# Two transposed tiles of the combine weights, moved from the expert stage to the start of the feed-forward stage

## The chip, the cores and the metric

The kernel runs on one core of a Trainium2 chip. The metric is the time of one execution on the device in microseconds (us), lower is better. Beside the timed runs there is one profiled execution, from which all rows of the trace come. TensorE is PE in the rows (PEld for its weight loads), VectorE is DVE, ScalarE is ACT, GpSimd is POOL, and SP issues the transfers.

## The reference

```python
x = attention(q, k, v)            # 4 batches, 8 heads, 576 tokens, head size 64; banded masks
# x: 2304 tokens x 512
logits = x @ phi                  # 2304 x 32 slots (8 experts, 4 slots each)
d = softmax(logits, axis=0); slot_input = d.T @ x
h = relu(slot_input[e] @ w1[e]);  slot_out[e] = h @ w2[e]       # for each expert e
c = softmax(logits, axis=1)       # the combine weights, 2304 x 32
x = c @ slot_out                  # 2304 x 512
h = x @ w_in                      # 512 -> 2048
r = relu(h);  g = r * r
out = g @ w_out                   # 2048 -> 512
```

## The kernel before

The order of the instructions on every engine is written out by hand, in two strings of tokens: `ATT` for the attention stage and the routing, `SEQ` for the rest. A loop at the end takes `SEQ` token by token and calls the function of each; an engine does its instructions in the order in which they were called. The letters behind a token say which engine does it (`A` ScalarE, `V` VectorE).

**Expert stage.** `y` multiplies a w1 tile (`L736`), `x` a w2 tile (`exp2`, `L859`); each tile is a transfer of 1 MB. `so` copies an expert group's result out of PSUM (`L873`), `sel` transposes it (`L764`) and copies it into `sT` (`L767`), which holds `slot_out` transposed.

**Feed-forward stage.** It never forms `c @ slot_out`. It forms M = `slot_out @ w_in` (32 rows) and then h = c @ M, by chunks of 128 columns of the 2048. So that the product keeps its precision in the fast format, the combine weights and M are held in three row groups, high parts and low parts: `C3` is the transposed combine weights, 96 rows, and M has 96 rows too.

- `cp ca.A cv` makes one of the eight tiles of `C3`, 288 columns each: `cp` three transposes on TensorE into a PSUM tile (`L702`), `ca` the copy into `C3` (`L713`), `cv` the subtraction that leaves the low part in rows 64 to 95 (`L718`, VectorE). The tiles 0 to 3 form `C3a`, the others `C3b`. After each `cp` GpSimd lays out the next tile's input in three copies (`L690`).
- `iM.0` to `iM.4` turn chunk M of w_in from 64 to 32 bits (`L806` or `L808`, `L812` on ScalarE, `L815`, `L819` and `L824` on VectorE), `oM` the same for w_out, and `sM` splits the w_out chunk into a high and a low part (`L839`, `L844`).
- `MM.0` to `MM.2` are the matmuls for chunk M of M (`L911`), the copy of the high part (`L923`), and the subtraction for the low part (`L934`).
- `h` is c @ M for 384 tokens (`L956`), `u` the relu (`L963`), `q` and `g` the square in two forms (`L971`, `L973`), `l` its low part (`L978`), `oa` and `ob` the matmuls with w_out (`L984`, `L990`), `e` the copy of a finished result.
- `w` followed by a number is as many filling matmuls, whose result nobody reads (`L759`). `P1` and `P2` change the memory pools.

The first `h` reads columns 0 to 383 of `C3a`, the tiles 0 and 1, and the second reads columns 384 to 767, the tiles 2 and 3 among them. Both read what M0's `L934` leaves. Before `P2` the transposes of a `C3` tile go into PSUM tiles of their own, and after it into one of the two banks `ph` that M and `h` use in turn.

Of the kernel before, what the change touches and what calls it, by code (L numbers as in the profile page):

```python
# [64 lines left out]
"""  # L65
SEQ = """
y i0.0A y y y i0.1A y y y y i0.2V r.A y y t.V y r.A cp ca.V cv y x r.A y y i0.3V t.V y x t.V y r.V x x x cp ca.V cv
o0.0A x x x x i0.4V x t.A o0.1A x cp ca.A cv x x o0.2V cp ca.A cv x o0.3V so.AV x x P1 so.A o0.4V s0.0V s0.1V sel.V
sel.A w2 P2 i1.0V i1.1A i1.2V i1.3V o1.1A M0.0 o1.0V i1.4V w4 M0.1A o1.2V M0.2V o1.3V i2.0A h h w2 u i2.2V i2.1A o1.4V
M1.0 q.A g.V s1.0A oa i2.3V M1.1A u s1.1V o2.1A M1.2V cp q.A l h g.A i2.4V ob ca.A l o2.0A oa cv u o2.2V i3.1A o2.3V  # L70
q.A h ob g.V i3.0A o2.4V M2.0 u o3.1A l oa s2.0V q.A M2.1V g.A s2.1V o3.0A M2.2V ob i4.1A i3.2V i3.3V h h oa l u u
i3.4V q.A o3.2V g.A ob o3.3V q.A l M3.0 g.A o3.4V i4.0A cp l oa M3.1V s3.0A i4.2V ca.A o4.1A M3.2V ob cv s3.1V o4.0A h
# [1075 lines left out]
```

## Time and profile before

| | us |
|---|---|
| median of 3 runs | 393.33 |
| lowest and highest of them | 391.93, 393.42 |
| the profiled execution | 391.63 |
| its span | 389.5 |
| TensorE busy in the span | 372.4 (96%) |
| VectorE busy | 259.8 (67%) |
| ScalarE busy | 228.2 (59%) |

The span is what the trace covers; the profiled execution's own time is 2.1 us longer. A busy share over the whole span is a mean over stages: attention until about 112 us, the expert stage until about 148, then the feed-forward stage, in which the weights are converted until about 245. A row of the trace names the line, the engine, the operation, what it writes and reads (`out<-in`), and behind `[` how long the engine stood idle before it and what ended that. Matmuls are pipelined and their bars overlap.

### The profile page before, as it was taken

The page shows a single profiled execution, that of the slowest core. Times are in us where ns is not written, and L with a number is a line of the kernel's source. Part 1 is how long each engine was busy: PE and PEld are TensorE (multiplying, and loading weights), DVE is VectorE, ACT ScalarE, POOL GpSimd, SP SyncE. Part 2 cuts the span into 40 slices and gives each one's busy share as a digit, 9 for nine tenths or more (in the row PEclk, how much of TensorE's full clock was granted, in tenths as well). Part 3 has the DMA queues.
Part 4 walks back from the last instruction along what each step waited for, and adds up shares of the span by engine and source line. Part 5 has one row for each costly group of instructions (what it writes and reads, how often), then busy time and mean ns, then how long its engine had stood idle before and what let it go on. Part 6 is the DMA issues. An engine that isn't in the chain of part 4 may idle for free.

```text
span 389.5 us, 8547 instructions
## 1 busy us (share of the span) xinstructions
PE 372.4 (96%) x3220; PEld 277.6 (71%) x3220; DVE 259.8 (67%) x594; ACT 228.2 (59%) x663; POOL 81.9 (21%) x166
## 2 busy tenths in 40 slices
PE   6888999999989998999999999999999999999996
PEld 2665777777653325878777777888888888888885
DVE  1577888989452238999999999564554455545554
ACT  3475878788433026998789786464444445544450
POOL 3798977874110010110000002000000000000000
PEclk9599999999999999999999999999999999999999
DMA  7999997779999999835354200040000000300004
GB/s 191 362 405 403 404 385 239 244 233 343 385 383 387 386 384 380 325 119 201 112 193 136 107 0 0 2 162 0 3 0 1 2 0 36 127 0 0 2 1 162
DMA packets 32584, 70.14 MB, mean 180 GB/s; under 512 B 2336, under 2 KB 6048, under 8 KB 32544
## 3 DMA queue, kind: packets, MB, share of 16 engines
q1 hardware_dynamic: 32544, 69.61, 50.0%
q8 instruction: 25, 0.41, 0.4%
q14 instruction: 15, 0.12, 0.1%
HBM read 64.88 MB, written 4.72 MB: 179 GB/s over the span
## 4 chain that ended last, share of the span: by engine, by line
PE 66%; DVE 20%; DMA 5%; issue 4%; ACT 2%; SPq 1%; DVEq 0%; ACTq 0%
PE acc L984 24%; PE acc L990 12%; PE o L403 5%; PE pt L389 5%; DVE cv L824 4%; PE psh L736 4%; DMA slotC<-in_w_dram 4%; DVE lo L978 3%; DVE slotA L819 3%; PE s L345 3%; PE ph L956 3%; PE xnp L444 3%; PE pacc L556 2%; DVE cv L815 2%; PE s L338 2%
## 5 line engine op out<-in xcount | busy, mean ns | idle before, releaser
L984 PE MATMUL acc<-wohl,hi 128*128 128x512 f32 x580 | 152.6, 396 | 0.0
L984 PEld LDWEIGHTS acc<-wohl,hi 128*128 128x128 f32 x580 | 107.3, 189 | 22.6 <-issue 0.8
L963 ACT ACTIVATE u<-ph 128x384 f32<-128x384 f32 x96 | 46.6, 493 | 70.9 <-PE ph L956 69.8
L990 PE MATMUL acc<-wohl,lo 128*128 128x512 f32 x290 | 84.9, 395 | 0.3
L973 DVE TENSOR_TENSOR g<-u 128x384 f32<-128x384 f32 x74 | 41.0, 557 | 55.3 <-ACT u L963 55.1
L990 PEld LDWEIGHTS acc<-wohl,lo 128*128 128x128 f32 x290 | 54.2, 188 | 13.7 <-DVE lo L978 1.2
L978 DVE TENSOR_TENSOR lo<-g,hi 128x384 fp32r<-128x384 f32 x96 | 52.8, 555 | 7.9
L370 ACT ACTIVATE p<-s,ns 128x96 f32<-128x96 f32 x144 | 46.8, 343 | 16.4 <-DVE ns L363 15.5
L971 ACT ACTIVATE hi<-u 128x384 fp32r<-128x384 f32 x82 | 43.0, 527 | 2.1
L381 POOL TENSOR_TENSOR p<-p,ns 128x288 f32<-128x288 f32 x48 | 31.1, 667 | 18.9 <-DVE ns L377 11.8
L690 POOL COPY c3n<-c_all 96x96 f32<-96x96 f32 x24 | 8.8, 401 | 113.1 <-PE ph L702 85.9
L370 ACT ACTIVATION_READ_ACCUMULATOR p<-s,ns 128x1 f32 x144 | 30.1, 209 | 0.0
L389 PE MATMUL pt<-ident,p 128*96 128x128 f32 x144 | 26.1, 292 | 1.0 <-DVE pts L394 0.8
L359 DVE TENSOR_REDUCE ns<-s 128x3 f32<-128x288 f32 x48 | 19.3, 442 | 4.9 <-PE s L345 4.9
L819 DVE SCALAR_TENSOR_TENSOR slotA<-slotA 128x1024 int32<-128x1024 int32 (+1 forms) x18 | 18.7, 1040 | 0.6 <-ACT slotA L812 0.5
L824 DVE CUSTOM_DVE_ANT_0 cv<-slotA,cv 128x2048 uint16<-128x2048 uint16 (+1 forms) x18 | 18.8, 1045 | 0.1
L389 PEld LDWEIGHTS pt<-ident,p 128*96 128x96 f32 x144 | 14.5, 130 | 6.1 <-issue 2.1
L956 PE MATMUL ph<-C3a,M 96*128 96x384 f32 x48 | 16.4, 351 | 2.0 <-DVE M L934 1.1
L224 POOL TENSOR_TENSOR slotC<-slotC,zero 32x384 f32<-32x384 f32 (+1 forms) x24 | 17.8, 746 | 2.3 <-DMA slotC<-in_vw_dram 1.6
L812 ACT ACTIVATE slotA<-slotA 128x1024 int32<-128x1024 uint32 (+1 forms) x18 | 18.0, 1006 | 0.0
L394 ACT COPY pts<-pt 96x384 f32<-96x384 f32 x23 | 10.9, 475 | 9.4 <-PE pt L389 9.4
L956 PE MATMUL ph<-C3b,M 96*128 96x384 f32 x48 | 16.3, 340 | 0.0
(173 smaller groups left out, 497.0 us busy)
## 6 DMA issues: line engine op xcount, KB each, us to landing
slotC<-in_w_dram SPq DMA_DIRECT2D x14, 1024.0 KB, 12.8
slotB<-in_w_dram SPq DMA_DIRECT2D x11, 1024.0 KB, 12.3
slotA<-in_w_dram SPq DMA_DIRECT2D x6, 1024.0 KB, 7.9
slotA<-in_w_in_dram SPq DMA_DIRECT2D x6, 1024.0 KB, 5.3
slotA<-in_w_out_dram SPq DMA_DIRECT2D x6, 1024.0 KB, 4.9
slotC<-in_kq_dram SPq DMA_DIRECT2D x6, 576.0 KB, 10.4
out_dram<-e SPq DMA_DIRECT2D x12, 256.0 KB, 2.3
slotB<-in_kq_dram SPq DMA_DIRECT2D x5, 576.0 KB, 8.1
```

Of the source, the lines that this page charges most:

```text
L370: nc.scalar.activation(p[:, i, :], s[:, i, :], AF.Exp, bias=ng[:, i:i + 1], scale=SCALE, accum_out=sm[:, i:i + 1])
L381: {"v": nc.vector, "g": nc.gpsimd}[e].tensor_tensor(p, p, rs.unsqueeze(2).to_broadcast([128, 3, KB]), op=ALU.mult)
L389: nc.tensor.transpose(pt[:, i, :], p[:, i, :], ident)
L819: nc.vector.scalar_tensor_tensor(w[:, :, 1], w[:, :, 1], -2 ** 31, w[:, :, 0], op0=ALU.bitwise_and, op1=ALU.bitwise_or)
L824: E[e].tensor_tensor(box["yi"], box["yi"], box["w"][:, :, 1], op=ALU.add)
L956: nc.tensor.matmul(t, lhsT=pools["M3"][:, 128 * fc:128 * fc + 128], rhs=C3[half][:, t0:t0 + GT], start=True, stop=True)
L963: nc.scalar.activation(r, u_t[k], AF.Relu)
L971: nc.scalar.activation(t, r, AF.Square)
L973: nc.vector.tensor_tensor(t, r, r, op=ALU.mult)
L978: nc.vector.tensor_tensor(lo, g_t.pop(k), hi_t[k], op=ALU.subtract)
L984: nc.tensor.matmul(a[:, c], lhsT=hi_t[k][:, sl], rhs=w[:, c], start=first, stop=False)
L990: nc.tensor.matmul(a[:, c], lhsT=lo_t[k][:, sl], rhs=wo_hl[fc][0][:, c], start=False, stop=last)
```

## The change

The tiles 2 and 3 of `C3` are made later. Their two groups `cp ca.A cv` leave the expert stage, where they stood between `x` tokens. The group of tile 2 goes right behind `P2`, before the rest of chunk 1's conversion and before `M0.0`. The group of tile 3 goes behind `i1.4V`, in front of the fillers there, which become two in place of four.

```diff
-o0.0A x x x x i0.4V x t.A o0.1A x cp ca.A cv x x o0.2V cp ca.A cv x o0.3V so.AV x x P1 so.A o0.4V s0.0V s0.1V sel.V
-sel.A w2 P2 i1.0V i1.1A i1.2V i1.3V o1.1A M0.0 o1.0V i1.4V w4 M0.1A o1.2V M0.2V o1.3V i2.0A h h w2 u i2.2V i2.1A o1.4V
+o0.0A x x x x i0.4V x t.A o0.1A x x x o0.2V x o0.3V so.AV x x P1 so.A o0.4V s0.0V s0.1V sel.V
+sel.A w2 P2 cp ca.A cv i1.0V i1.1A i1.2V i1.3V o1.1A M0.0 o1.0V i1.4V cp ca.A cv w2 M0.1A o1.2V M0.2V o1.3V i2.0A h h w2 u i2.2V i2.1A o1.4V
```

On VectorE, from the copy into `sT` on, this stood before (`slotA_72` is the first chunk of w_in and w_out that comes through the ring, `cv` its converted form, `M` and `ph` those of M0):

```order
L767 COPY sT<-pht 128x12x16
L808 TENSOR_SCALAR cv<-slotA_72 128x512
L815 TENSOR_SCALAR cv<-cv 128x512
L819 SCALAR_TENSOR_TENSOR slotA_72<-slotA_72 128x512
L808 TENSOR_SCALAR cv<-slotA_72 128x512
L824 ISA cv<-slotA_72,cv 128x1024
L815 TENSOR_SCALAR cv<-cv 128x512
L934 TENSOR_TENSOR M_2667<-ph_2674,M_2667 32x128
```

And this stands there now:

```order
L767 COPY sT<-pht 128x12x16
L718 TENSOR_TENSOR C3a<-ph_2654,C3a 32x3x96
L808 TENSOR_SCALAR cv<-slotA_72 128x512
L815 TENSOR_SCALAR cv<-cv 128x512
L819 SCALAR_TENSOR_TENSOR slotA_72<-slotA_72 128x512
L808 TENSOR_SCALAR cv<-slotA_72 128x512
L824 ISA cv<-slotA_72,cv 128x1024
L718 TENSOR_TENSOR C3a<-ph_2654,C3a 32x3x96
L815 TENSOR_SCALAR cv<-cv 128x512
L934 TENSOR_TENSOR M_2647<-ph_2655,M_2647 32x128
```

The two subtractions `L718` now stand between the copy into `sT` and M0's `L934`; nothing else on VectorE changes its place among the others.

On TensorE, between the last `x` and the first `h`, before:

```order
L859 MATMUL pso<-slotC_89,h1T 32x512 x4
L764 MATMUL pht<-ident,so 128x128 x8
L759 MATMUL warm<-C3a 128x384 x2
L911 MATMUL ph_2674<-cv_2393,sT 96x128 x4
L759 MATMUL warm<-C3a 128x384 x4
L956 MATMUL ph_2675<-C3a,M_2667 128x384
```

And now:

```order
L859 MATMUL pso<-slotC_89,h1T 32x512 x4
L764 MATMUL pht<-ident,so 128x128 x8
L759 MATMUL warm<-C3a 128x384 x2
L702 MATMUL ph_2654<-ident,c3n 96x96 x3
L911 MATMUL ph_2655<-cv_2393,sT 96x128 x4
L702 MATMUL ph_2654<-ident,c3n 96x96 x3
L759 MATMUL warm<-C3a 128x384 x2
L956 MATMUL ph_2655<-C3a,M_2647 128x384
```

Three transposes now stand on either side of M0's matmuls (`L911`), which go into the other `ph` bank than before; the fillers behind M0 are two.

## Rows read from the trace of the kernel before

**Rows 1.** The page, parts 1 and 2: span, and TensorE's clock in 40 slices.

```profile
span 389.5 us, 8547 instructions
...
PEclk9599999999999999999999999999999999999999
```

**Rows 2.** The chain of waits, 110 to 260 us: start, length, what.

```profile
132.20 14.28 DMA slotC<-in_w_dram
...
147.65 0.59 ACT so L873
...
149.20 0.68 ACT slotA L812
...
151.90 0.28 DVE M L934
...
240.31 0.96 PE acc L990 x3
```

**Rows 3.** The timeline of TensorE, 140 to 153 us: start, length, instruction.

```profile
140.92 0.45 PE L702 MATMUL c3p<-ident,c3n 96*96 96x96 f32 x3
...
146.52 1.07 PE L859 MATMUL pso<-slotC,h1T 128*32 128x512 f32 x8 [1.05 <-DMA slotC<-in_w_dram]
...
148.70 0.60 PE L759 MATMUL warm<-C3a 96*128 96x384 f32 x2
149.36 1.11 PE L911 MATMUL ph<-cv,sT 128*96 128x128 f32 x8
...
152.24 0.62 PE L956 MATMUL ph<-C3a,M 96*128 96x384 f32 x2 [1.06 <-DVE M L934]
```

**Rows 4.** The timeline of the other engines, 136 to 159 us.

```profile
136.72 0.70 ACT L806 ACTIVATE cvo<-wo 128x512 f32<-128x512 f32 x1 [10.70 <-DVE cv L824]
...
141.41 0.39 ACT L713 CAST C3a<-c3p 96x288 fp32r<-96x288 f32 x1 [0.52 <-PE c3p L702]
...
141.84 0.46 DVE L718 TENSOR_TENSOR C3a<-c3p,C3a 32x288 fp32r<-32x288 f32 x1 [5.15 <-ACT C3a L713]
...
142.32 0.43 DVE L815 TENSOR_SCALAR cvo<-cvo 128x512 int32<-128x512 int32 x1
...
148.21 0.36 DVE L767 COPY sT<-pht 128x192 f32<-128x192 f32 x1 [0.72 <-PE pht L764]
...
148.49 0.42 DVE L808 TENSOR_SCALAR cv<-slotA 128x512 f32<-128x512 f32 x1
...
148.94 0.43 DVE L815 TENSOR_SCALAR cv<-cv 128x512 int32<-128x512 int32 x1
...
149.90 0.69 DVE L819 SCALAR_TENSOR_TENSOR slotA<-slotA 128x512 int32<-128x512 int32 x1 [0.54 <-ACT slotA L812]
...
151.45 0.42 DVE L815 TENSOR_SCALAR cv<-cv 128x512 int32<-128x512 int32 x1
...
156.29 1.47 POOL L690 COPY c3n<-c_all 96x96 f32<-96x96 f32 x3 [11.87 <-PE ph L702]
...
158.15 0.43 DVE L815 TENSOR_SCALAR cv<-cv 128x512 int32<-128x512 int32 x1
...
158.50 0.69 DVE L819 SCALAR_TENSOR_TENSOR slotA<-slotA 128x512 int32<-128x512 int32 x1
```

**Rows 5.** Busy time by stretch: stretch, length, PE, PEld, DVE, ACT, POOL, clock, DMA.

```profile
152.20:240.30 88.10, 86.82 (x447) 68.45 (x447) 87.10 (x142) 75.05 (x141) 5.36 (x9) 1.00 0.43 148
240.30:300.00 59.70, 59.69 (x273) 48.74 (x274) 32.12 (x58) 29.89 (x63) 0.00 (x0) 1.00 0.07 27
```

**Rows 6.** TensorE's waits, 20 to 389 us: sum, times, longest.

```profile
PE ph L956 <- DVE M L934: 1.1, 1, 1.1
```

**Rows 7.** The timeline of TensorE, 6 to 12 us.

```profile
8.74 0.45 PE L338 MATMUL s<-cb 64*64 64x288 bf16 x3 [2.20 <-ACT p L370]
```

**Rows 8.** Busy time by stretch, at the start of the span.

```profile
8.50:9.00 0.50, 0.26 (x5) 0.25 (x6) 0.00 (x0) 0.50 (x5) 0.00 (x0) 0.50 1.02 310
18.00:18.50 0.50, 0.50 (x17) 0.50 (x17) 0.21 (x1) 0.50 (x5) 0.50 (x3) 0.50 0.97 396
```

## The prediction

> **What bounds the kernel now.** I read the page first [rows 1]: TensorE's clock is full but for the first slices, so the question is where TensorE still waits. The chain of waits around the change comes next [rows 2]. The reader should see three things in it. The expert stage ends on a transfer: the last w2 tile is under way from 132.20, for 14.28 us. Then the chain hops over short steps, the copy of `so` on ScalarE at 147.65 and, behind the transposes that follow it, i1.1 at 149.20, the `L812` of the first w_in chunk. From there it stays on VectorE up to the second half of M0 (`L934`, 151.90), which releases the first `h`.
>
> TensorE's rows say the same from the other side [rows 3]. The last matmuls of the expert stage begin at 146.52 after 1.05 us of waiting for the transfer, and the first `h` begins at 152.24 after 1.06 us of waiting for `L934`. That second wait is what I call the hole. The single steps on ScalarE and VectorE [rows 4] show what fills it: after its copy into `sT` (148.21) VectorE goes through `L808`, `L815`, waits 0.54 us for ScalarE's `L812`, and does `L819` at 149.90.
>
> Last the stretch behind the hole [rows 5]: of the 88.1 us from 152.2 to 240.3, VectorE is busy 87.10 and TensorE 86.82. Both run without slack. What is lost in the hole isn't given back on the way, unless one of them finds the 1.0 or 1.3 us that are left.
>
> **What leaves the expert stage.** Two groups of three transposes (`L702`), each 0.45 us [rows 3] (the row at 140.92); two copies on ScalarE of 0.39 us; two subtractions on VectorE (`L718`) of 0.46 us [rows 4] (the rows at 141.41 and 141.84). TensorE gets back up to 0.9 us, but ahead of a wait for a transfer that ends when it ends: the wait before 146.52 grows from 1.05 to about 1.9. ScalarE and VectorE get back time too, but VectorE's next step that counts, the copy into `sT`, waits for TensorE at 148.21 anyway (0.72 us of waiting). So the removal is worth 0. If the transfer were not the cover, it would be worth up to 0.9.
>
> **What arrives in the hole.** Three sums, one for each engine.
>
> TensorE: the transposes of tile 2 stand between the two fillers and M0. The fillers' bars run from 148.70 to 149.30; bars overlap, so I start the transposes at about 149.15 (bounds 148.95, and 149.36, where M0 began before). With 0.45 they end at 149.60. M0 moves from 149.36 by about 0.2 us, which doesn't decide anything. The second group replaces two fillers, behind M0, and needs tile 3's copies on GpSimd; the same three copies took 1.47 us beside a busy VectorE [rows 4] (the row at 156.29), so 149.60 + 1.47 + 0.45 gives 151.5 at the latest.
>
> ScalarE: its copy of tile 2 stands ahead of i1.1 (`L812`). It begins 0.04 us behind the transposes, as in the expert stage (140.92 + 0.45 to 141.41), lasts 0.39 and ends at 150.03. `L812` begins at about 150.0 instead of 149.20 and ends at about 150.7.
>
> VectorE: the subtraction of tile 2 (`L718`) is now the first thing behind the copy into `sT`. It can't begin before ScalarE's copy has ended, at 150.06. VectorE works in the order written: in the expert stage `L718` waited 5.15 us for ScalarE's copy, and `L815` on `cvo`, whose operand was there at 136.72 + 0.70 = 137.42, ran only behind it, at 142.32 [rows 4]. Here the same wait runs from the end of the `sT` copy, 148.21 + 0.36 = 148.57, to 150.06, 1.5 us with nothing done, and queued behind it are `L808` and `L815` of the first chunk, which before ran in this very time. From 150.06 I go on with measured steps: `L718` to the next instruction 0.48 (141.84 to 142.32), `L808` to `L815` 0.45 (148.49 to 148.94), `L815` to `L819` 0.35 (158.15 to 158.50). `L819` is at 151.34, where it was at 149.90: +1.44. ScalarE's `L812` has ended by then, so the old wait of 0.54 us is gone; it is already in this sum. The subtraction of tile 3 stands ahead of `L815` and M0's `L934` and adds 0.48. ScalarE's copy for it is done at about 151.5 + 0.4 = 151.9, and VectorE comes to it at 151.34 + (151.45 - 149.90) = 152.9, so it doesn't wait there.
>
> The sum: 1.44 + 0.48 = **1.9 us** later for `L934`, and so the first `h` at 152.24 + 1.92 = 154.16. With the bounds on where the transposes start it is 1.7 to 2.1. VectorE's work behind it is the same as before and leaves it 1.0 us idle in 88.1 [rows 5], so I take nothing off; if all that both engines have left were used, 1.3 us of TensorE's, the bound below would be 0.6. From 240.3 on VectorE is busy for about half of the time and TensorE for nearly all [rows 5], so a later start there is a later end.
>
> The profiled execution took 391.63 us, its span 389.5 [rows 1]. By the sum the span becomes 391.4 and the execution 393.5. The three timed runs have their median at 393.33, 1.7 over the profiled one, and the lowest of them at 391.93; so I put the sum on the median, 393.33 + 1.9 = **395.2**, and keep 393.5 inside the range.
>
> **The clock.** Before, TensorE's longest waits between 20 and 389 us for ScalarE's or VectorE's work were those of 1.1 us like the hole [rows 6], and its clock stayed full [rows 1]. Now it has nothing from the end of the fillers, about 152.0 (151.5 and two fillers), to 154.16: some 2.2 us. The one fall of the clock in this trace came with a wait of that size: 2.20 us without a matmul before 8.74 [rows 7], the clock at 0.50, that is 1.2 GHz, from 8.5, and still there at 18 to 18.5 [rows 8]. Here matmuls follow the wait almost without a break [rows 5], so I hold a fall possible, not likely.
>
> The Trainium skill ("TensorE: Matmul & The Clock Gate", Part 1) says that the clock's resting state is the half rate, and that only activity holds it at full. Its Part 4 says that the full clock "doesn't engage" for transposes, which would make them poor fillers and speaks against this change. By that rule the hole would be the fourth case below; by the rows it is the first. The trace doesn't decide it: the clock is full from the third slice on [rows 1], but no stretch there is transposes alone.
>
> **The rivals.**
>
> 1. *The order on VectorE decides* (the forecast): +1.9, 395.2. Chance 0.62.
>
> 2. *The loss is taken back* (the not-slower side): the hole is late by 1.9, but the next 88 us absorb it, because TensorE's weight loads and VectorE's buffers have run ahead further than their busy shares show. It decides at the wait before `acc` at 240.31: if that step is late by less than 0.6, this is it. For it: the chain hops between both engines without a long wait. Against: the 87.10 and 86.82 of 88.1. Time: +0 to +0.6, 393.3 to 393.9. Chance 0.18.
>
> 3. *The expert stage ends earlier*: if the last w2 tile did land earlier, because the matmuls give back their slots sooner, the 0.9 us of transposes would be saved and half of the loss gone: +1.0; with VectorE's stall covered as well, -0.9, 392.4. Against: that transfer is under way from 132.20 [rows 2], and the first transposes to go stand at 140.92 [rows 3], behind its issue. Chance 0.07.
>
> 4. *The clock falls in the hole*: TensorE would do the stretch after 154 at half rate. At the start the half rate lasted from 8.5 to 18.5, 10 us, which would cost 5.0 us of work here; with an early return about none. Halfway, 2.5, gives +4.4, 397.7; at most 400.2. Chance 0.13.
>
> **How the numbers follow.** What a measurement can tell from no change is about 0.5%, 2.0 us: 395.3 and 391.4 are the edges. The forecast lies just under the upper edge, with 395.0 to 395.4 by its own bounds and 393.5 if the timed runs come down to the profiled one; I give four tenths of its chance to "slower", 0.25, and 0.37 to "same". The fourth rival adds 0.13 less 0.01 for an early return; the second and 0.04 of the third, which by its price lies inside the edges, count as same; 0.03 of the third stays for a gain that I have priced too low. Slower 0.37, same 0.60, faster 0.03. The range leaves out most of the fourth rival and the end of the third: 392.7 to 397.2. The likeliest's own range is 393.5 to 395.6.
>
> **What would show it.** In the changed profile `L718` (`C3a<-ph`) stands on VectorE at about 150.1 with 1.5 us of waiting for ScalarE's `L713` before it; `L819` of the first chunk at 151.3; the first `h` at 154.2 with 2.2 us of waiting for `L934`; the wait for the last w2 tile at 1.9 us; and the end of the conversions, the `acc` at 240.31, later by 1.7 to 2.1. The forecast is wrong if the first `h` comes before 153.5, if `L718` doesn't wait, if the lateness at 240 is under 1 us, or if the granted clock is below 1.00 anywhere from 146 to 165.

## The result and the profile after

The changed kernel took 395.52 us (median of 12 runs, 393.83 to 398.18), the kernel before 393.49 (12 runs, 391.79 to 395.67): a ratio of 1.0051, 95% interval 1.0028 to 1.0075. Measured again beside the experiments it was 395.90 against 392.47, 1.0084 (1.0057 to 1.0111). By the medians the change costs 2.0 us in the first measurement and 3.4 in the second. The forecast was 395.2.

The profiled execution is the longest of its 12 runs, 398.18. Its page, first the span and TensorE's clock in 40 slices [rows 1]:

```profile
span 396.2 us, 8546 instructions
...
PEclk9579999999978999899999999999999999999999
```

Two losses of clock stand ahead of the changed place: the start and the end of attention (slices 2 to 3 and 12 to 13). The start differs from run to run of the kernel before too (half rate for 10.2 us in its first profile, 13.6 in its second), and the loss at the end of attention is missing in the changed kernel's second profile, so I don't compare spans. I count from an event behind both, the first transposes of `so` (`L764`): 151.43 here, and before, in the timeline of [rows 3], 147.52:

```profile
147.52 1.43 PE L764 MATMUL pht<-ident,so 128*128 128x128 f32 x8
```

The chain of waits from there on:

```profile
151.56 0.59 ACT so L873
...
153.49 0.40 ACT C3a L713
...
153.92 0.06 DVE C3a L718
...
154.40 0.44 DVE cv L808
...
155.21 0.75 DVE slotA L819
...
157.06 0.47 DVE C3a L718
...
158.00 0.29 DVE M L934
...
158.34 0.96 PE ph L956 x2
```

Where the chain went from `so` to i1.1's `L812` [rows 2], it now goes through ScalarE's copy of tile 2 and both subtractions. TensorE's timeline (the answer to [rows 3]):

```profile
150.43 1.07 PE L859 MATMUL pso<-slotC,h1T 128*32 128x512 f32 x8 [0.73 <-DMA slotC<-in_w_dram]
151.43 1.43 PE L764 MATMUL pht<-ident,so 128*128 128x128 f32 x8
...
153.04 0.41 PE L702 MATMUL ph<-ident,c3n 96*96 96x96 f32 x3
...
154.52 0.42 PE L702 MATMUL ph<-ident,c3n 96*96 96x96 f32 x3
154.72 0.60 PE L759 MATMUL warm<-C3a 96*128 96x384 f32 x2
158.34 0.96 PE L956 MATMUL ph<-C3a,M 96*128 96x384 f32 x2 [3.02 <-DVE M L934]
```

The wait before the first `h` has grown from 1.06 to 3.02 us. VectorE and GpSimd there (the answer to [rows 4]):

```profile
152.12 0.36 DVE L767 COPY sT<-pht 128x192 f32<-128x192 f32 x1 [2.98 <-PE pht L764]
153.92 0.46 DVE L718 TENSOR_TENSOR C3a<-ph,C3a 32x288 fp32r<-32x288 f32 x1 [1.44 <-ACT C3a L713]
...
155.21 0.75 DVE L819 SCALAR_TENSOR_TENSOR slotA<-slotA 128x512 int32<-128x512 int32 x1
155.88 0.48 DVE L808 TENSOR_SCALAR cv<-slotA 128x512 f32<-128x512 f32 x1
156.29 0.74 DVE L824 CUSTOM_DVE_ANT_0 cv<-slotA,cv 128x1024 uint16<-128x1024 uint16 x1
157.06 0.46 DVE L718 TENSOR_TENSOR C3a<-ph,C3a 32x288 fp32r<-32x288 f32 x1
...
158.00 0.28 DVE L934 TENSOR_TENSOR M<-ph,M 32x128 fp32r<-32x128 f32 x1
```

```profile
153.59 0.68 POOL L690 COPY c3n<-c_all 96x96 f32<-96x96 f32 x3 [12.52 <-PE ph L702]
155.08 1.41 POOL L690 COPY c3n<-c_all 96x96 f32<-96x96 f32 x3 [0.81 <-PE ph L702]
```

`L718` waits 1.44 us for ScalarE, as the forecast has it. `L819` is 3.78 us behind the transposes of `so` (before 2.38: +1.40), `L934` 6.57 (4.38: +2.19), the first `h` 6.91 (4.72: +2.19). The busy times by stretch (the answer to [rows 5]):

```profile
158.00:159.00 1.00, 0.66 (x2) 0.66 (x3) 0.97 (x3) 0.00 (x0) 0.00 (x0) 0.71 1.05 387
159.00:160.00 1.00, 1.00 (x5) 0.87 (x5) 1.00 (x4) 0.98 (x3) 0.00 (x0) 0.50 1.05 401
160.00:161.00 1.00, 1.00 (x6) 1.00 (x6) 1.00 (x2) 1.00 (x3) 0.00 (x0) 0.50 1.03 410
161.00:162.00 1.00, 1.00 (x6) 0.91 (x5) 0.73 (x3) 0.34 (x3) 0.00 (x0) 0.58 0.90 313
...
158.34:246.60 88.26, 87.35 (x447) 69.99 (x447) 86.77 (x141) 74.63 (x141) 4.73 (x9) 0.98 0.40 136
```

The granted clock is 0.50, the 1.2 GHz level, right behind the hole, for 0.58 + 2 + 0.84 = 3.4 us (a mean of 0.71 in a slice of 1 us is 0.58 us at half). And the last wait of the conversions:

```profile
247.00 0.97 PE L990 MATMUL acc<-wohl,lo 128*128 128x512 f32 x3 [0.16 <-DVE lo L978]
```

It is 95.57 us behind the transposes of `so`, before 92.79 [rows 2]: +2.78, and the end of the span +2.79 (244.77 against 241.98). So 2.2 us arise in the hole, and 0.6 behind it.

### The profile page after: what moved, and what is told of

It reads as the page before. It is cut to its first block, busy times and chain, and to the rows that moved or that the text cites. A ratio compares the mean times of both kernels' runs of the same rounds, so it can differ in the third digit from the quotient of the medians.

```text
span 396.2 us, 8546 instructions
## 1 busy us (share of the span) xinstructions
PE 376.7 (95%) x3218; PEld 280.9 (71%) x3218; DVE 261.1 (66%) x594; ACT 227.8 (58%) x663; POOL 82.0 (21%) x166
## 3 DMA queue, kind: packets, MB, share of 16 engines
HBM read 64.88 MB, written 4.72 MB: 176 GB/s over the span
## 4 chain that ended last, share of the span: by engine, by line
PE 66%; DVE 19%; DMA 5%; issue 4%; ACT 4%; SPq 1%; DVEq 0%; ACTq 0%
PE acc L984 23%; PE acc L990 12%; PE o L403 5%; PE pt L389 5%; PE psh L736 4%; DMA slotC<-in_w_dram 4%; DVE cv L824 4%; PE ph L956 3%; DVE lo L978 3%; PE s L345 3%; DVE slotA L819 3%; PE pacc L556 2%; PE xnp L444 2%; ACT p L370 2%; DVE cv L815 2%
## 5 line engine op out<-in xcount | busy, mean ns | idle before, releaser
L389 PE MATMUL pt<-ident,p 128*96 128x128 f32 x144 | 26.9, 299 | 1.7 <-DVE pts L394 1.6
L824 DVE CUSTOM_DVE_ANT_0 cv<-slotA,cv 128x2048 uint16<-128x2048 uint16 (+1 forms) x18 | 18.8, 1044 | 0.1
L819 DVE SCALAR_TENSOR_TENSOR slotA<-slotA 128x1024 int32<-128x1024 int32 (+1 forms) x18 | 18.8, 1045 | 0.0
L812 ACT ACTIVATE slotA<-slotA 128x1024 int32<-128x1024 uint32 (+1 forms) x18 | 17.9, 1002 | 0.2 <-DMA slotA<-in_w_in_dram 0.2
L403 PE MATMUL o<-pts,slotC 96*64 96x64 f32 x288 | 15.3, 244 | 1.4 <-ACT pts L394 1.4
```

Source lines behind the costliest of these rows:

```text
L389: nc.tensor.transpose(pt[:, i, :], p[:, i, :], ident)
L403: nc.tensor.matmul(o[64 * h:64 * h + 64, j, :], lhsT=v_t[u][:, 3 * c + j, 64 * h:64 * h + 64], rhs=pt_t[2 * n + h][:, j, QB * i:QB * i + Q ...
L819: nc.vector.scalar_tensor_tensor(w[:, :, 1], w[:, :, 1], -2 ** 31, w[:, :, 0], op0=ALU.bitwise_and, op1=ALU.bitwise_or)
L824: E[e].tensor_tensor(box["yi"], box["yi"], box["w"][:, :, 1], op=ALU.add)
```

## The experiments

All offsets count from the start of the transposes of `so` in the same profile; "+" is against the kernel before (first `h` 4.72, end of the span 241.98).

**The two profiles again.** `e_after` is the changed kernel unchanged, `e_before` the kernel before unchanged.

> The changed kernel itself, beside the others and on their chip. Theory A: 2.0 us longer than before, ratio 1.004 to 1.006; from the copy into sT to M0's L934 5.9 us, where before had 3.69; the granted clock falls to half for some 3 us behind the hole in most executions, at a cost of about 0.5 us. Theory B (the clock makes the loss): an execution in which the clock does not fall there is as short as before.

> The kernel before, unchanged, for a second profile. If its rows around the change are typical: first h 4.7 us behind the first transposes of so, with about 1.1 us of waiting for L934, granted clock 1.00 behind it, and the span's end 242.0 us behind those transposes (241.7 to 242.3). If the clock fell behind this hole too, the half clock that the changed kernel shows there would not be its longer hole's doing.

`e_after`: first `h` 6.92 with 3.02 us of waiting, end +2.75, clock at half behind the hole. `e_before`: first `h` 4.72, end 242.04. Its TensorE and the clock behind it:

```profile
153.28 0.62 PE L956 MATMUL ph<-C3a,M 96*128 96x384 f32 x2 [1.07 <-DVE M L934]
```

```profile
154.50:155.50 1.00, 1.00 (x9) 1.00 1.00 375
```

The clock stays full behind the hole of before in both profiles, and both accounts repeat to 0.06 us. That is what lets differences of some tenths be read below, where the times can't. The ratio of `e_after`, 1.0084, is above the 1.004 to 1.006 expected; its theory B is settled by `e_fill` below, where the clock doesn't fall.

**One group at a time.** `e_first` moves only tile 3's group, to the first place; `e_second` only that group, to the second.

```diff
-o0.2V cp ca.A cv x o0.3V
+o0.2V x o0.3V
-sel.A w2 P2 i1.0V
+sel.A w2 P2 cp ca.A cv i1.0V
```

```diff
-o0.2V cp ca.A cv x o0.3V
+o0.2V x o0.3V
-o1.0V i1.4V w4 M0.1A
+o1.0V i1.4V cp ca.A cv w2 M0.1A
```

> Only one tile moves: tile 3 goes right behind P2, ahead of i1.0; tile 2 stays in the expert stage, and the four fillers behind i1.4 stay. Theory A (the order on VectorE): L718 waits some 1.4 us for ScalarE's copy, L819 of the first chunk and the first h are 1.4 us later than before, the time 1.4 us longer, ratio about 1.0037. Theory B (the fall of the clock in the longer hole makes the loss): the hole grows from 1.1 to about 2.5 us, so the loss comes only where the clock falls, and the time is longer by under 0.7 us on the median.

> Only one tile moves: tile 3 goes behind i1.4, with two fillers in place of four; tile 2 stays in the expert stage. Theory A: VectorE comes to the subtraction at about 151.5, ScalarE's copy is done by then or 0.3 us later, so only its 0.48 us are added: first h 0.5 to 0.8 us later, ratio 1.0012 to 1.002. Theory B: the hole stays near 1.5 us, no fall, no loss.

`e_first`: first `h` +1.39, end +1.89; 395.08 us, ratio 1.0057 (1.0036 to 1.0078). `e_second`: first `h` +0.61, end +1.23; 393.99 us, 1.0009 (0.9988 to 1.0029). The 1.39 and 0.61 add up to 2.00. Both are by theory A. Most of the loss hangs on the first place, where VectorE comes to the subtraction before ScalarE has made its operand; in the second place it finds it ready:

```profile
153.42 0.46 DVE L718 TENSOR_TENSOR C3a<-ph,C3a 32x288 fp32r<-32x288 f32 x1 [1.44 <-ACT C3a L713]
```

```profile
155.04 0.46 DVE L718 TENSOR_TENSOR C3a<-ph,C3a 32x288 fp32r<-32x288 f32 x1
```

**More fillers.** `e_fill` is the changed kernel with 14 fillers in place of 2 ahead of `M0.1A`.

```diff
-cp ca.A cv w2 M0.1A
+cp ca.A cv w14 M0.1A
```

> The changed kernel with 14 fillers in place of 2 behind the second moved tile, so that TensorE works through the hole: some 2 us more of matmuls that nobody reads. Theory A: VectorE's stall is untouched, the first h stays 1.9 to 2.2 us late, the granted clock stays 1.00 around it, and the time is 1.9 us longer than before, ratio 1.004 to 1.005. Theory B: with the clock held the loss is gone or under 0.7 us.

```profile
157.48 0.62 PE L956 MATMUL ph<-C3a,M 96*128 96x384 f32 x2 [0.93 <-DVE M L934]
...
245.60 0.96 PE L990 MATMUL acc<-wohl,lo 128*128 128x512 f32 x3 [0.20 <-DVE lo L978]
```

```profile
158.00:159.00 1.00, 0.94 (x7) 1.00 1.03 393
159.00:160.00 1.00, 1.00 (x8) 1.00 1.05 414
```

With TensorE idle for 0.93 us only, the clock stays full. The first `h` is at +2.21 all the same, the `acc` at +2.26 (95.05), the end at +2.17. This settles two things. The stall is passed on whole, nothing of it is taken back in 88 us. And the fall of the clock is worth the rest, 2.77 (the mean of the changed kernel's two profiles) - 2.17 = 0.6 us. The time, 395.74 us, 1.0062 (1.0038 to 1.0085), can't tell this 0.6 from nothing.

**The work without the wait.** `e_cvonly` is the kernel before with its two subtractions moved behind `sel`, and without the two fillers there.

```diff
-cp ca.A cv x x o0.2V cp ca.A cv x
+cp ca.A x x o0.2V cp ca.A x
-sel.A w2 P2
+sel.A cv cv P2
```

> The kernel before, in which only the two subtractions L718 of the tiles 2 and 3 are moved: from the expert stage to the place directly behind the copy into sT. Their transposes and ScalarE copies stay in the expert stage, so nothing can be waited for; the two fillers behind sel are dropped. Theory A (what costs in the changed kernel is VectorE's work and, above all, its wait for ScalarE): only the work is left, 2 x 0.48 = 0.96 us, of which the old wait of 0.54 us before L819 takes up its share, so that the first h is later by about 0.4 us (0.3 to 0.6) and the end with it; time +0.4 us. Rival B (any work added behind sT counts in full, the wait is beside the point): first h and end +1.0 us.

```profile
149.84 0.83 DVE L718 TENSOR_TENSOR C3a<-c3p,C3a 32x288 fp32r<-32x288 f32 x2
...
151.50 0.69 DVE L819 SCALAR_TENSOR_TENSOR slotA<-slotA 128x512 int32<-128x512 int32 x1
...
152.44 0.69 DVE L824 CUSTOM_DVE_ANT_0 cv<-slotA,cv 128x1024 uint16<-128x1024 uint16 x1
153.04 0.42 DVE L815 TENSOR_SCALAR cv<-cv 128x512 int32<-128x512 int32 x1
```

```profile
153.83 0.62 PE L956 MATMUL ph<-C3a,M 96*128 96x384 f32 x2 [1.42 <-DVE M L934]
```

```profile
154.00:155.00 1.00, 0.95 (x5) 1.00 1.08 388
155.00:156.00 1.00, 1.00 (x7) 0.59 1.04 393
156.00:157.00 1.00, 1.00 (x5) 0.50 1.02 395
```

The first `h` is at +0.36, by theory A. But the end is at +0.97, which looks like rival B and isn't: behind a wait of 1.42 us the clock fell again, at 155.2, and the 0.6 between both numbers is of the size of the 0.6 of `e_fill`. I had not put the clock into this expectation. Time 393.43 against 393.07, ratio 1.0018 (0.9996 to 1.0041).

**Taking the wait apart.** `e_nowait` keeps both groups late, but lets ScalarE do i1.1 first and spreads the subtractions.

```diff
-P2 cp ca.A cv i1.0V i1.1A i1.2V
+P2 cp i1.0V i1.1A ca.A i1.2V
-i1.4V cp ca.A cv w2 M0.1A o1.2V M0.2V
+i1.4V cv cp M0.1A ca.A w2 o1.2V M0.2V cv
```

> The changed kernel with the same work in the feed-forward stage, but ordered so that VectorE meets no wait of 1.4 us: the transposes of tile 2 stay behind P2, ScalarE's copy comes behind i1.1, the subtraction behind i1.4; tile 3's transposes follow, and its subtraction stands behind M0's L934. Theory A: the 1.44 us of stall go, 0.96 us of subtractions stay on VectorE, plus up to 0.2 us of waiting before the second: first h 0.5 us later than before, i.e. the time 1.0 to 1.2 us longer than before and about 0.8 us shorter than with the change, ratio about 1.003. Theory B: no long hole, no fall of the clock, the time of before.

```profile
153.61 0.79 DVE L819 SCALAR_TENSOR_TENSOR slotA<-slotA 128x512 int32<-128x512 int32 x1 [0.55 <-ACT slotA L812]
```

```profile
156.03 0.42 PE L702 MATMUL ph<-ident,c3n 96*96 96x96 f32 x3 [1.86 <-DVE C3a L718]
```

The wait for `L713` is gone; `L819` (2.40 behind the transposes) is where it was before. The first `h` is at +0.78, but a new wait came: the transposes of tile 3 need the `ph` bank that the subtraction of tile 2 frees. The second subtraction waits 0.26 us, the `L819` of o1.3 is 1.50 later from the copy into `sT` on, where I expected 1.0 to 1.2, and the clock falls to half from 157.6 on. The end is at +1.61. The time, 395.68 us, 1.0068 (1.0042 to 1.0093), shows no gain over the changed kernel; though its trace has 1.2 us less of lateness. The stretch from the first w1 matmul to the transposes of `so` was longer in its profile (35.42 us; 34.58 and 35.05 in those of the changed kernel), and I can't say why.

**GpSimd's part.** `e_rep` is the changed kernel with four `c3n` tiles; the copies for the tiles 0 to 3 are made at the start.

```diff
-        t = c3n_t[i] = late.tile([96, 3, 3, NS], F32, tag="c3n", name="c3n")
+        k = (0, 1, 2, 3, 0, 1, 0, 1)[i]
+        t = c3n_t[i] = late.tile([96, 3, 3, NS], F32, tag=f"c3n{k}", name="c3n")
...
-        if i < 2 * B - 1:
-            c3_rep(i + 1)
+        if i in NEXT:
+            c3_rep(NEXT[i])
...
-    c3_rep(0)
+    for i in range(4):
+        c3_rep(i)
+    NEXT = {0: 4, 1: 5, 4: 6, 5: 7}
```

> The changed kernel, in which GpSimd lays out the inputs of the first four tiles at the start (four c3n tiles instead of one), so that it makes none of these copies between the copy into sT and the first h. Theory A (the copies of 0.68 and 1.41 us beside VectorE lengthen VectorE's steps there, which is what makes the lateness 2.2 us instead of the 1.9 summed up): L819 of the first chunk 0.69 us instead of 0.75, the second L808 0.42 instead of 0.48, L824 0.69 instead of 0.74, the L718 of tile 2 still waits about 1.4 us, and the first h is 6.6 to 6.7 us behind the first transposes of so instead of 6.9. Rival B (these lengths come from something else, such as the transfers): the steps stay at 0.75, 0.48 and 0.74 and the first h at 6.9.

Its lines carry other numbers (`L822` is `L819`, `L811` `L808`, `L827` `L824`, `L719` `L718`); its transposes of `so` begin at 149.48:

```profile
151.97 0.46 DVE L719 TENSOR_TENSOR C3a<-ph,C3a 32x288 fp32r<-32x288 f32 x1 [1.44 <-ACT C3a L714]
...
153.26 0.69 DVE L822 SCALAR_TENSOR_TENSOR slotA<-slotA 128x512 int32<-128x512 int32 x1
153.86 0.42 DVE L811 TENSOR_SCALAR cv<-slotA 128x512 f32<-128x512 f32 x1
154.20 0.69 DVE L827 CUSTOM_DVE_ANT_0 cv<-slotA,cv 128x1024 uint16<-128x1024 uint16 x1
154.92 0.46 DVE L719 TENSOR_TENSOR C3a<-ph,C3a 32x288 fp32r<-32x288 f32 x1
```

Theory A holds: 0.69, 0.42 and 0.69 in place of 0.75, 0.48 and 0.74. From `L819` to the second subtraction it is 1.66 us, in the changed kernel 1.85; the first `h` is at 6.72, a little above the 6.6 to 6.7 expected. One run, 395.88 us.

**Other places for the tiles.** `e_late` leaves the groups in the expert stage, but as late as it goes. `e_early` makes the tiles 4 to 6 there as well, which takes a ring slot (`RING_C` 7 in place of 8) for an early `C3b`; `e_ring7` takes only the slot.

```diff
-x cp ca.A cv x x o0.2V cp ca.A cv x o0.3V so.AV x x P1
+x x x o0.2V x o0.3V so.AV x cp ca.A cv cp ca.A cv x P1
```

```diff
-RING_A, RING_B, RING_C, RING_D = 5, 8, 8, 1
+RING_A, RING_B, RING_C, RING_D = 5, 8, 7, 1
```

> The kernel before with the two groups still in the expert stage, but as late as can be: both stand between the last two w2 tiles, in TensorE's wait for the last transfer. Theory A: what leaves the middle of the expert stage is worth 0, so this is the time of before within 0.3 us, ratio 0.999 to 1.001, and from the copy into sT to L934 it is 3.7 us as before. Theory C (their old places in the expert stage cost time, or VectorE's conversion of chunk 0 there ends later and matters): 0.5 us or more either way.

> The opposite of the change: on top of the four tiles of before, the tiles 4, 5 and 6 are made in the expert stage too (C3b is allocated earlier, and the ring of weight tiles loses one of its 22 slots to make room). Theory A: three subtractions of 0.48 us leave the stretch in which VectorE has no slack, three groups of transposes of 0.38 leave TensorE's there, and go where both engines wait for transfers: 1.0 to 1.4 us shorter than before, ratio 0.9965 to 0.9975, unless TensorE's 1.2 us more in the expert stage exceed its waits there. If only the hole were sensitive and not the whole stretch behind it, the time would be that of before.

> Control for the kernel with the early tiles: the kernel before with the ring of weight tiles at 21 slots in place of 22, nothing else. Theory A: the transfers bound the expert stage at the same rate, 0 to 0.3 us longer, ratio 1.000 to 1.001.

`e_late` missed: the end is at +0.57, 394.04 us, 1.0025 (0.9998 to 1.0052). VectorE's rows tell why:

```profile
149.77 0.46 DVE L718 TENSOR_TENSOR C3a<-c3p,C3a 32x288 fp32r<-32x288 f32 x1 [3.19 <-ACT C3a L713]
151.09 0.46 DVE L718 TENSOR_TENSOR C3a<-c3p,C3a 32x288 fp32r<-32x288 f32 x1 [0.87 <-ACT C3a L713]
151.58 0.69 DVE L824 CUSTOM_DVE_ANT_0 cvo<-wo,cvo 128x1024 uint16<-128x1024 uint16 x1
...
153.49 0.36 DVE L767 COPY sT<-pht 128x192 f32<-128x192 f32 x1
```

The late subtractions hold up o0's conversion, and that the copy into `sT`: 1.94 us behind the transposes of `so` in place of 0.69. VectorE has only the 0.72 us of waiting before `L767` [rows 4] to spare there. `e_early` ends at -1.24, by theory A, but takes 393.99 us, 1.0027 (1.0004 to 1.0050), because the missing slot alone costs more: `e_ring7` 395.82 us, 1.0074 (1.0049 to 1.0100), where 1.000 to 1.001 was expected. In its profile the clock was at half as well, from 146.2 to 153.1, mostly ahead of the changed place.

`e_part` makes the tiles 4 and 5 in the expert stage without that slot, with `C3b` split in two buffers (768 and 384 columns; tiles 6 and 7 in two pieces each).

```diff
-cv y x r.A y y i0.3V
+cv y x cp ca.V cv r.A y y i0.3V
-o0.0A x x x x i0.4V
+o0.0A x x x cp ca.V cv x i0.4V
...
+    C3[1] = late.tile([96, 768], F32R, name="C3b")
...
-        C3[1] = mp1.tile([96, NT // 2], F32R, name="C3b")
+        C3[2] = mp1.tile([96, 384], F32R, name="C3c")
```

> The kernel before, turned the other way: two more tiles (4 and 5) are made in the expert stage instead of leaving it. For room C3b is split in two buffers of 768 and 384 columns, the first of which exists early, and tiles 6 and 7 are written and subtracted in two pieces. Theory A (VectorE's work behind the transposes of so sets the end, and work ahead of them is free as long as it is early enough): two subtractions of 0.48 us leave the VectorE-bound stretch and about 0.3 us of pieces come in; end minus start of those transposes 0.5 to 0.7 us less than before, time about 0.6 us less. Rival B (the expert stage has no room for this work, as the late placing of the subtractions there showed): the last w2 tile is multiplied later, and the time is the same or up to 1 us more.

First `h` 4.73, end 241.17 (-0.81, somewhat more than the 0.5 to 0.7 expected); 392.29 us against 393.07, ratio 0.9983 (0.9960 to 1.0005). The trace is by theory A, and its median is the lowest of the study against the kernel before, but the times don't set it apart from that kernel.

## Why the prediction was right, and where not

**VectorE's order: right.** The step that carried the forecast is there row for row: 1.44 us of waiting before `L718` (forecast 1.5), `L819` later by 1.40 (1.44). `e_first` without the second place keeps 1.39 of it; `e_cvonly`, with the same two subtractions but their operands ready, only 0.36.

**The second subtraction: mis-sized.** "Adds 0.48" became 2.19 - 1.40 = 0.79, which puts the first `h` outside the stated 1.7 to 2.1. Of it 0.48 is the step. 0.12 is that the instruction behind `L824` begins 0.60 us after it, before its 0.69 us are over, when it is `L815` (152.44 to 153.04 in `e_cvonly`), and 0.72 us after it, when they are over, when it is the subtraction (154.20 to 154.92 in `e_rep`); I took the distance from the subtraction to the instruction behind it, and not the one ahead of it. 0.19 is GpSimd (6.91 against 6.72 in `e_rep`): its copies for the next tile, a part of `cp`, now run beside VectorE and lengthen three of its steps. I had priced those copies only as something that the transposes wait for.

**TensorE's wait: mis-sized.** 3.02 us for the 2.2 forecast. 0.3 of the difference is the first `h` itself, which was that much later than forecast. The rest lies at the other end: GpSimd's copies for tile 3 took 0.68 us, not the 1.47 of [rows 4], which I had used as the latest, so the second transposes and the fillers were done 0.6 us earlier, 3.9 us behind the transposes of `so` in place of 4.5, and the hole began there.

**The clock: the fourth rival's mechanism came on top.** I called the fall possible, not likely, and took a granted clock below 1.00 as a sign that the forecast is wrong; it fell in both profiles. The forecast's sum has no term for it. What failed with it is that rival's price: 2.5 us on top of the 1.9, while `e_fill` puts it at 0.6. 0.8 of the difference is the length, 3.4 us at half rate where the rival's middle case has 5. The other 1.1 is that the rival counts TensorE's lost work as lost time: of 3.4 us at half rate TensorE loses 1.7 us of work, and only 0.6 arrive at the end. That fits a VectorE that sets the pace in this stretch [rows 5]; no run shows it by itself.

**The loss isn't taken back: right,** and the second rival refuted: +2.21 at the first `h`, +2.17 at the end in `e_fill`. The `acc` at the end of the conversions was to be later by 1.7 to 2.1; with the clock held it is 2.26 later, and in the changed kernel, with the fall, 2.78.

**The removal is worth 0: the sign for it was useless.** The wait for the last w2 tile was to grow from 1.05 to 1.9; it is 0.73, and 1.66 in `e_after`. In `e_before` it is 0.68 where the first profile of the same kernel has 1.05: it moves with the transfer from one execution to the next. No profile shows a gain from the removal. A cost isn't excluded: from the first w1 matmul to the transposes of `so` it is 33.97 and 33.60 us in the two profiles of the kernel before, 34.58 and 35.05 in those of the changed one. But in `e_cvonly`, whose transposes stay, it is 34.68. What the removal is worth stays open.

**The sum against the time.** By the trace 2.2 + 0.6 = 2.8 us; the two measurements have 2.0 and 3.4. Fitted over 193 timed runs, with one price for each microsecond at half clock (0.19 us, worked out from each run's mean clock), the two sets of the changed kernel stand 2.2 and 2.3 us above those of the kernel before at equal clock, and 3.4 us of half clock make 0.19 x 3.4 = 0.6 more. That agrees with the trace in both parts, and leaves little for a cost of the removal. That the 395.2 came out within 0.3 us of 395.52 is in part luck: the sum leaves out 0.3 us of the hole and 0.6 of the clock, 0.9 us that the trace shows, and the first measurement's difference came out 0.8 below the trace's.

## What to carry to other kernels

A filler for one engine brings its company along: here three free transposes brought a copy on ScalarE, a subtraction on VectorE and copies on GpSimd, and the hole belonged to VectorE. Before something is moved into an engine's idle time, ask whose work the idle time waits for, and where in that engine's order the new instructions stand: 0.46 us of work cost 1.4 us because it stood first and its operand was late. Work ahead of a fixed event is free only up to the slack of the tightest engine there (0.7 us in `e_late`).

## What the runs showed of the chip

- The granted clock fell behind TensorE's waits of 1.42, 1.75, 2.46, 2.82 and 3.02 us before the first `h` (`e_cvonly`, `e_second`, `e_first`, `e_rep`, both profiles of the changed kernel) and behind one of 1.86 ahead of tile 3's transposes (`e_nowait`), and not behind those of 0.93, 1.06, 1.07, 1.08, 1.09 and 1.22 (`e_fill`, both of before, `e_part` and `e_ring7`, `e_late`, `e_early`). But the length of one wait doesn't decide it: waits of 1.65 and 1.66 us for a w2 tile, in the expert stage, left the clock full (`e_after`, `e_nowait`, `e_rep`, `e_early`), and in `e_ring7` the clock fell at the end of one of 1.65. The fall came when matmuls were running again, from 0.1 us after the wait's end (the changed kernel's first profile) to 1.6 us after it (`e_rep`). I had compared the wait with the 2.20 us at the start [rows 7] alone.
- Three copies on GpSimd took 0.68 us where VectorE was idle or in `L718`, and 1.41 beside `L819`, `L808` and `L824`, which took 0.05 to 0.06 us more each. The Trainium skill ("SBUF — State Buffer", Who interferes with whom) says that a VectorE instruction with two SBUF inputs contends with GpSimd's reads, and that the one that starts later is blocked until the other has finished. The trace agrees for `L819`, which reads two tensors: the second of the three copies, 0.26 us long at the median, lasted from 155.36 to 156.08 in the first profile, past the end of `L819` at 155.96. That sentence doesn't speak of `L808`, which reads one tensor and took 0.06 us more as well.
- One of the 22 slots for 1 MB tiles less cost 2.9 us by the ratio (`e_ring7`, 1.0074).
